# Storing the attention outputs of the first two sequences at other steps of the item loop

## The chip, the cores and the metric

The kernel runs on one core of a Trainium2 chip. The metric is the device time of one execution in microseconds (us); the time given for a kernel is the median of its runs.

## What is computed

The reference is an attention block of the RWKV-5 kind (a recurrent state for each head, decayed by w at each token) followed by a mixture of experts that uses one expert for a token. Cut to what matters:

```python
# r, k, v: (B, H, S, D) = (4, 8, 768, 48); w, u: (H, D)
for t in range(S):
    cur = einsum('bhd,bhe->bhde', u * k[t], v[t])
    y[t] = einsum('bhd,bhde->bhe', r[t], state + cur)
    state = w * state + einsum('bhd,bhe->bhde', k[t], v[t])
x = y as (B, S, H * D)                      # 4 x 768 tokens of 384
logits = x @ w_gate                         # 8 experts
e[s] = argmax(logits[s]) if s == 0 or sigmoid(x[s] @ w_local) < 0.5 else e[s - 1]
out[s] = softmax(logits[s])[e] * (relu(x[s] @ w1[e]) @ w2[e])
```

x, the attention's output, is the array whose storing the change moves. The kernel keeps it in device memory as `x_d` (3072 rows of 384 float32), because the experts later gather its rows by token number.

## The kernel before

**Stages.** First comes attention (0 to about 107 us), with the routing of the first two sequences woven in; then the experts (to the end of the span at 380 us), with the routing of the other two woven into the first expert units. The order of the work on each engine is written out by hand: the program is emitted under `manual_schedule`, and each engine runs its instructions in the order of the code. The framework adds the semaphores.

**Items and steps.** Attention works on 16 items, an item being one sequence b and one pair of heads hp (n = 4 b + hp). `Attention.run` (L352) is a loop over steps n = 0 to 16. A regular step does, in this order: `load(n + 3)` puts three DMAs on SP's queue (rk, kv and vT of a later item); `turn(n - 2)` transposes the outputs of item n - 2 on TensorE and copies them on ScalarE (ACT) into the tile `x` of their sequence (L329, L331); `added` and `states` form the states between chunks; `scale(n + 1)` is three multiplies on GpSimd (POOL), rw, ke and pd; `inside(n - 1)` and `before(n - 1)` finish the products of item n - 1 on TensorE, and `before` ends with one ACT copy from PSUM into `xT` (L318); two calls of `scores` (L288) and their masking on VectorE (DVE, L290) follow for the item ahead; `own(n)` (L267, L273) begins the outputs of item n in PSUM; `keys` is one more DVE multiply. Where n is a multiple of 4, `logits` (L342, L343) multiplies the gate's weights with the outputs of the sequence that has just been finished.

**Where the stores are.** An item's outputs are turned two steps after its own, so the four items of sequence b are all in `x` after `turn` of step 4 b + 5. There, at the end of `turn`, L334 stores the whole sequence, 768 rows of 1536 bytes, with one DMA on ACT's queue: for the first sequence in step 5, the second in step 9, the third in step 13, the fourth after the loop. ACT issues it right after the copies that it depends on.

**Buffers.** `x` has two buffers (L305): the third sequence's tile is the first's again, and the fourth's is the second's. The first write into the third sequence's tile is the pair of copies of `turn(8)` in step 10, into the fourth's that of `turn(12)` in step 14. These copies have to wait until the store that reads the old contents has landed. The PSUM for the transposes comes from two pairs of banks that every user takes in turn (`banks`, L184): in a regular step `turn` takes one, the first `scores` the other, the second `scores` the first one again. The outputs of `own` have a single tile `y`, which the ACT copy into `xT` must have read before `own` of the next item writes it.

**Loads.** Four buffers each hold rk and vT and five hold kv, so SP issues a load as soon as its buffer is free, up to three steps ahead of the loop.

**Readers of x_d.** `heads()` in step 15 is the first gather (L1083, POOL), from the rows of the first two sequences. Later gathers read all rows.

Of the kernel before, what the change touches and what calls it, by code (L numbers as in the profile page):

```python
# [20 lines left out]
P = 128  # L21
B, H, S, DH = 4, 8, 768, 48
HP = H // 2
# [38 lines left out]
class Attention:  # L62
# [260 lines left out]
    def turn(self, n, banks):  # L323

        nc, b, h0 = self.nc, self.items[n]["b"], 2 * self.items[n]["hp"]
        x = self.xs[b]
        for h in range(2):
            for c2 in range(C2):
                nc.tensor.transpose(banks[h][:, c2 * P:c2 * P + U], self.outputs(b, h0 + h)[:U, c2 * P:(c2 + 1) * P], self.ident[:U, :U])  # L329
        for h in range(2):  # L330
            nc.scalar.copy(x[:, :, (h0 + h) * DH:(h0 + h + 1) * DH],  # L331
                           banks[h][:, :C2 * P].rearrange("p (c e) -> p c e", e=DP)[..., :DH])
        if h0 == H - 2:
            nc.scalar.dma_start(out=self.x_d[b * S:(b + 1) * S, :].rearrange("(c p) d -> p c d", p=P), in_=x)  # L334

    def logits(self, b, bank):

# [14 lines left out]
    def run(self, router, fetch, heads):  # L352
# [11 lines left out]
        for n in range(M + 1):  # L364
# [69 lines left out]
            if n == g + 3:  # L434

                router.turn_runs(0, mp[:, mp_end:])
            self.before(n - 1)
            if M - 2 <= n < M:
                fetch(2 * (n - M + 2) + 1)
            if n == 6:  # L440
# [478 lines left out]
def route(tc, once, ps, lt, ident, gates):  # L919
# [57 lines left out]
    nc.vector.tensor_copy(ccol, cp[:NC, :1])  # L977
    run = tl("run", [NC, P])
    nc.vector.tensor_tensor_scan(run, rows, rows, ccol, Alu.max, Alu.max)
    rp = bank("rp")  # L980
    nc.tensor.transpose(rp[:, :NC], run, ident[:NC, :NC])
    ei = tl("ei", [P, NC], I32)
    nc.vector.tensor_copy(ei, rp[:, :NC])
# [15 lines left out]
class Experts:  # L999
# [49 lines left out]
    def fetch(self, i, engine):  # L1049
        u, wp = self.units[i], self.wps[i % 2]  # L1050
        if i < EARLY:
            w1, w2 = self.w1[u["e"]], self.w2[u["e"]]
        else:
            e = self.nc.values_load(self.router.order[0:1, i - EARLY:i - EARLY + 1], engines=[ET.SP], min_val=0, max_val=E - 1,
                                    skip_runtime_bounds_check_because="the blocks' experts are a permutation")
            w1, w2 = [w[bass.ds(e, 1)].rearrange("o p x -> (o p) x") for w in (self.w1, self.w2)]
        u["w1"] = wp.tile([P, FK, DK, P], F32, name="w1t", tag="w1t")
        engine.dma_start(out=u["w1"].rearrange("p m k f -> p (m k f)"), in_=w1)
        u["w2"] = wp.tile([P, FK, D], F32, name="w2t", tag="w2t")
        engine.dma_start(out=u["w2"].rearrange("p m f -> p (m f)"), in_=w2)  # L1060
# [691 lines left out]
```

## Time and profile before

| what | us |
|---|---|
| median of three runs | 381.67 (381.08 to 381.85) |
| the profiled execution, whole | 382.02 |
| its span, first to last instruction | 380.2 |
| PE busy in the span | 366.5 (96%) |
| DVE, POOL, ACT busy | 249.2, 151.2, 107.2 |
| ACT starts to issue the four stores at | 40.35, 64.70, 90.31, 114.80 |
| one issue on ACT | 0.38 to 0.40 |
| `before`'s ACT copy (L318) of steps 8, 9, 10, 12 starts at | 59.73, 67.34, 72.62, 84.46 |
| copies of `turn(8)`, `turn(12)` start at | 69.83, 94.96 |
| first gather starts at | 106.41 |

How to read it: PE is TensorE's matmuls, PEld its weight loads, DVE VectorE, ACT ScalarE, POOL GpSimd, SP the engine that issues the loads. A line of the timeline has the start, the duration, engine and source line, the operation with its output and input tiles, how many, and in square brackets how long the engine sat idle before and what ended that. A line of the waits has the waiting instruction, what it waited for, the total in us, how often, and the longest. The rows of slices cut the span into 40 equal parts of 9.5 us and give a busy share in tenths. "DMA to landing" is the time from the issue of a DMA to its completion. The DMA queues are told apart too: q1 holds SP's loads, q10 the DMAs that ACT issues.

### The profile page before, as it was taken

To read this page: it belongs to the slowest core of one execution; us is meant where nothing else is said; L and a number is where in the kernel's file an instruction comes from. 1 tells how busy PE (TensorE), PEld (TensorE's weight loads), DVE (VectorE), ACT (ScalarE), POOL (GpSimd) and SP (SyncE) were. 2 spreads that over 40 slices of the span, in tenths; PEclk is the share of its full clock that TensorE was granted. 3 is DMA by queue.
4 is the path that set the end of the run, shared out by engine and by line. 5 is a ranking of instruction groups with operands and counts; after the bars stand their busy time and mean duration, and the time that the engine had idled before them with its cause. 6 is when DMAs were issued, how large, how long until landed. Compare 5 with 4: busy or idle time off the path is not lost. (4 is left out here: it accounts for less than half of the span.)

```text
span 380.2 us, 9697 instructions
## 1 busy us (share of the span) xinstructions
PE 366.5 (96%) x3846; PEld 323.6 (85%) x3846; DVE 249.2 (66%) x720; ACT 107.2 (28%) x295; POOL 151.2 (40%) x213
## 2 busy tenths in 40 slices
PE   8899999999999999999999999999999999999992
PEld 7676777776769989999999999999898899899971
DVE  6988778889853736587557857757658758466400
ACT  4132232232322112223323233233233233232210
POOL 7699999896222043211423213223323123012022
PEclk9999999999999999999999999999999999999997
DMA  7999999973738872811561254146146156063011
GB/s 255 413 411 407 409 395 338 378 276 128 246 121 288 331 275 72 320 53 39 202 219 42 68 222 174 35 174 228 56 167 232 34 181 228 12 225 161 3 37 36
DMA packets 17765, 74.97 MB, mean 197 GB/s; under 512 B 2761, under 2 KB 6618, under 8 KB 15408
## 3 DMA queue, kind: packets, MB, share of 16 engines
q1 hardware_dynamic: 10336, 56.89, 40.0%
q0 software_dynamic: 3424, 9.52, 7.5%
q10 hardware_dynamic: 3952, 7.87, 5.8%
q8 instruction: 32, 0.52, 0.6%
q14 instruction: 21, 0.17, 0.2%
HBM read 64.83 MB, written 9.51 MB: 196 GB/s over the span
## 5 line engine op out<-in xcount | busy, mean ns | idle before, releaser
L1309 POOL DMA_INDIRECT out_dram<-yo,sid x27 | 26.6, 986 | 102.2 <-ACT yo L1304 78.7
L1160 PE MATMUL h<-exT,w1t 128*128 128x168 f32 (+4 forms) x240 | 54.9, 327 | 0.0
L1164 DVE TENSOR_TENSOR hT<-h,hs 128x168 f32<-128x168 f32 (+3 forms) x60 | 21.1, 351 | 46.1 <-PE h L1160 30.5
L1083 POOL DMA_INDIRECT xg<-x_d,gid x29 | 31.2, 1076 | 36.2 <-DVE sm L906 17.4
L1160 PEld LDWEIGHTS h<-exT,w1t 128*128 128x128 f32 x240 | 41.6, 190 | 0.3 <-issue 0.3
L1110 PE MATMUL h<-exT,w1t 128*128 128x192 f32 (+1 forms) x192 | 38.3, 338 | 0.0
L1229 PE MATMUL y<-factors,sums 128*128 128x192 f32 x168 | 36.8, 326 | 0.0
L290 DVE TENSOR_TENSOR am<-pair,kept 128x768 f32<-128x768 f32 x32 | 29.9, 952 | 8.9 <-PE pair L288 8.7
L1160 PE MATMUL h<-xs,ws 128*128 128x168 f32 (+4 forms) x144 | 35.2, 326 | 0.0
L216 POOL TENSOR_TENSOR pd<-rk 128x384 f32<-128x384 f32 x32 | 31.4, 1003 | 7.7 <-PE y L267 5.5
L1110 PEld LDWEIGHTS h<-exT,w1t 128*128 128x128 f32 x192 | 32.3, 190 | 1.5 <-issue 0.2
L1160 PEld LDWEIGHTS h<-xs,ws 128*128 128x128 f32 x144 | 25.5, 190 | 4.3 <-ACT hs L1167 1.0
L1229 PEld LDWEIGHTS y<-factors,sums 128*128 128x128 f32 x168 | 28.9, 190 | 0.0
L212 POOL TENSOR_TENSOR ke<-kv,endT 128x288 f32<-128x288 f32 x32 | 24.9, 800 | 1.8 <-DMA kv<-in_kv_dram 1.8
L297 PE MATMUL y<-am,kv 128*64 128x128 f32 x360 | 22.8, 276 | 1.3 <-DVE y L273 1.2
L229 POOL TENSOR_TENSOR rw<-rk,tab 128x384 f32<-128x384 f32 x26 | 23.7, 936 | 0.2 <-DMA rk<-in_rk_dram 0.2
L288 PE MATMUL pair<-rw,kw 48*64 48x128 f32 (+1 forms) x768 | 23.0, 249 | 0.4
L1229 PE MATMUL y<-w2t,hT 128*128 128x192 f32 x96 | 23.0, 328 | 0.0
L1097 DVE COPY exT<-tp 128x384 f32<-128x384 f32 (+6 forms) x29 | 14.0, 489 | 13.6 <-PE tp L1096 13.4
L288 PEld LDWEIGHTS pair<-rw,kw 48*64 48x64 f32 x768 | 19.5, 133 | 2.6 <-POOL ke L212 0.6
L318 ACT COPY xT<-y 128x768 f32<-128x768 f32 x15 | 12.0, 799 | 33.6 <-PE y L310 33.6
L297 PEld LDWEIGHTS y<-am,kv 128*64 128x64 f32 x360 | 19.4, 137 | 2.4 <-DVE y L273 1.7
(301 smaller groups left out, 739.2 us busy)
## 6 DMA issues: line engine op xcount, KB each, us to landing
w1t<-in_w_dram SPq DMA_DIRECT2D x8, 1536.0 KB, 6.7
w2t<-in_w_dram SPq DMA_DIRECT2D x8, 1536.0 KB, 7.2
rk<-in_rk_dram SPq DMA_DIRECT2D x15, 768.0 KB, 9.1
kv<-in_kv_dram SPq DMA_DIRECT2D x16, 584.0 KB, 7.9
vT<-in_vT_dram SPq DMA_DIRECT2D x16, 384.0 KB, 10.0
x_d<-x ACTq DMA_DIRECT2D x4, 1152.0 KB, 9.5
w1t<-in_w_dram SPq DMA_DIRECT2D x2, 768.0 KB, 5.9
w2t<-in_w_dram SPq DMA_DIRECT2D x2, 768.0 KB, 5.4
```

The source lines that it names most:

```text
L212: nc.gpsimd.tensor_mul(t["ke"][:, p::2], t["k"][:, p::2], spread(self.endT[:, p, hp], 1, C2))
L216: nc.gpsimd.tensor_mul(t["pd"][:, z], t["rT"][:, z], t["kT"][:, z])
L229: engine.tensor_mul(t["rw"][:, z], t["rT"][:, z], spread(pw, 1, z.stop - z.start))
L288: nc.tensor.matmul(sc[f * DP:(f + 1) * DP, h, i, x:], lhsT=t["kw"][q, c, o * DP:(o + 1) * DP], rhs=t["rw"][q, c, x:], start=True, stop=True)
L290: return lambda: nc.vector.tensor_mul(t["am"][:, g], sc, spread(self.kept[:, g:g + 3], 1, 2))
L297: nc.tensor.matmul(t["y"][h][p * DP:(p + 1) * DP, c2 * P:(c2 + 1) * P], lhsT=t["v"][:, (2 * c + h) * DH:(2 * c + h) * DH + DP], rhs=t["am" ...
L1083: self.nc.gpsimd.indirect_dma_start(out=xg[:n], out_offset=None, in_=self.x_d[:rows], in_offset=bass.IndirectOffsetOnAxis(ap=u["gid"][:n, ...
L1110: nc.tensor.matmul(h[:, :n], lhsT=u["w1"][:, m, kk, :], rhs=u["xT"][:, kk, :], start=(kk == 0), stop=(kk == DK - 1))
L1160: nc.tensor.matmul(out, lhsT=a, rhs=b, start=start and k == 0, stop=stop and k == len(terms) - 1, skip_group_check=True)
L1164: nc.vector.tensor_tensor(out, a, b, op=Alu.add)
L1229: return lambda: nc.tensor.matmul(bank[:, x * half:(x + 1) * half], lhsT=a, rhs=b, start=(j == 0 and x == 0), stop=(j == FK // 2 - 1), ski ...
L1309: self.nc.gpsimd.indirect_dma_start(out=out.rearrange("n (h d) -> (n h) d", h=2) if half else out, out_offset=bass.IndirectOffsetOnAxis(ap ...
```

## The change

The store is taken out of `turn` into a function of its own, and `turn` calls it for the third and the fourth sequence alone. In the steps n = 8 and n = 12 the loop calls it, right after `before(n - 1)`, for the sequences 0 and 1. So the first sequence's store moves from step 5 to step 8, the second's from step 9 to step 12, both still on ACT's queue, now behind the copy into `xT` (L318) and ahead of the one of `logits` (L343). No instruction is added or taken away.

```diff
@@ turn
             nc.scalar.copy(x[:, :, (h0 + h) * DH:(h0 + h + 1) * DH],
                            banks[h][:, :C2 * P].rearrange("p (c e) -> p c e", e=DP)[..., :DH])
-        if h0 == H - 2:
-            nc.scalar.dma_start(out=self.x_d[b * S:(b + 1) * S, :].rearrange("(c p) d -> p c d", p=P), in_=x)
+        if h0 == H - 2 and b >= 2:
+            self.store(b)
+
+    def store(self, b):
+        self.nc.scalar.dma_start(out=self.x_d[b * S:(b + 1) * S, :].rearrange("(c p) d -> p c d", p=P), in_=self.xs[b])
@@ run
             self.before(n - 1)
+            if n in (2 * HP, 3 * HP):
+                self.store(n // HP - 2)
```

## Prediction

> **What bounds the kernel now.** I read the page's slices first, then busy time by stretch, the waits, and at last the timelines of ACT and PE around the places where the stores stand and where they are to go. The page's rows for TensorE and the DMA engines (40 slices of 9.5 us):
>
> ```profile
> PE   8899999999999999999999999999999999999992
> DMA  7999999973738872811561254146146156063011
> ```
>
> TensorE is nine tenths busy nearly from start to end, so anything that stops it shows in the time. The DMA engines are full only up to about 85 us, the attention stage, in which the four stores to x_d lie. Busy time by stretch there (one step of the loop is some 5.5 us; columns: length, busy us of PE, PEld, DVE, ACT, POOL, clock, DMA share, GB/s):
>
> ```profile
> 33.00:39.60 6.60, 6.26 (x149) 3.97 (x147) 5.03 (x7) 1.28 (x2) 6.60 (x9) 1.00 1.02 409
> 39.60:45.80 6.20, 6.14 (x132) 4.79 (x132) 4.00 (x24) 1.52 (x4) 6.20 (x8) 1.00 1.02 407
> 56.90:64.00 7.10, 7.10 (x148) 4.83 (x149) 6.20 (x8) 2.01 (x5) 7.10 (x9) 1.00 0.95 349
> 64.00:69.80 5.80, 5.80 (x131) 4.53 (x131) 3.27 (x8) 1.64 (x4) 4.13 (x6) 1.00 0.95 337
> 69.80:75.75 5.95, 5.95 (x149) 4.85 (x151) 5.88 (x11) 1.50 (x3) 5.95 (x8) 1.00 1.03 388
> 81.70:89.60 7.90, 7.90 (x168) 5.75 (x169) 6.94 (x10) 2.24 (x6) 7.49 (x9) 1.00 0.24 82
> ```
>
> Up to 64 us GpSimd has no idle time at all, from 57 us on TensorE has none; ACT is idle three quarters of the time. The clock is 1.00 throughout. From 40 us on no engine waits for a load: the last such wait is in the stretch 28 to 40 us, before the first store is issued,
>
> ```profile
> POOL ke L212 <- DMA kv<-in_kv_dram: 0.7, 1, 0.7
> ```
>
> So in these stretches the DMA engines are full, but not the bound. The issue of the first store, and landings in us by stretch, in an answer for 40 to 41 us and one for 80 to 100 us:
>
> ```profile
> L334 ACTq DMA_DIRECT2D x_d<-x x1: 400/400/400, 40.4 to 40.4; - x1
> DMA to landing us min/median/max: 14.4/14.4/14.4
> ```
> ```profile
> L334 ACTq DMA_DIRECT2D x_d<-x x1: 378/378/378, 90.3 to 90.3; - x1
> DMA to landing us min/median/max: 4.6/4.6/4.6
> ```
>
> The same 1152 KB take 14.4 us among loads and 4.6 us alone. That spread is what this change turns on.
>
> **What is taken out at steps 5 and 9.** Two issues, 0.40 us at 40.35 and 0.39 us at 64.70 on ACT. Behind them ACT is idle until 43.28 and 66.18, waiting for PE and DVE, so nothing is late there: gain 0. Their transfers leave two full stretches. The loads get about 3 us of DMA time back in 40 to 55 us (1.18 MB at 0.41 MB/us), but no one waits for them there, and GpSimd, which sets the pace, does the same 5.5 us of multiplies for an item: 0. One wait of SP's own is tied to the first store: in 50 to 55 us SP waits 0.8 us for x_d before a vT issue, and then 2.5 us more for a DVE multiply at L273 which is to free the buffer, so that too is worth 0. An upper bound for what I do not see: TensorE's idle time between 39.6 and 85 us. By stretch it is 0.06, 0.12, 0.12, 0, 0, 0 and 0.59 us, to 81.7 us; if all 0.9 us went, that would be the gain.
>
> **What is added at step 12.** The second store is issued after the copy at 84.46, so at 85.26. ACT's next work is at 87.43, after 2.17 us of waiting for PE, which hides the 0.4 us. From 85 to 90 us the DMA share is 0.01, so the price is that of the store at 90.31: landing at 85.26 + 4.6 = 89.9. Its buffer is written again by the copies at 94.96 (step 14, the first of the fourth sequence), 5.1 us later, and the gather that reads x_d starts at 106.41. Cost 0. Only the 14.4 us row would be too late here, by 99.7 - 94.96 = 4.7 us, and the reason for that row, the loads, is gone by then.
>
> **What is added at step 8.** This is the part that can cost. ACT's lines from the step 8 copy to the step 10 copies, and PE's of step 10:
>
> ```profile
> 59.73 0.80 ACT L318 COPY xT<-y 128x768 f32<-128x768 f32 x1 [2.09 <-PE y L310]
> 63.26 0.48 ACT L343 COPY lT<-pair 128x384 f32<-128x384 f32 x1 [2.73 <-PE pair L342]
> ...
> 69.83 0.70 ACT L331 COPY x<-pair 128x288 f32<-128x288 f32 x2 [1.69 <-PE pair L329]
> 72.62 0.80 ACT L318 COPY xT<-y 128x768 f32<-128x768 f32 x1 [2.09 <-PE y L310]
> ```
> ```profile
> 69.00 0.79 PE L329 MATMUL pair<-ident,xT 112*128 112x112 f32 x6
> ...
> 72.31 1.27 PE L288 MATMUL pair<-rw,kw 48*64 48x128 f32 x46
> 73.47 0.88 PE L267 MATMUL y<-pd,w_t 48*64 48x384 f32 x8
> ```
>
> The issue falls at 59.73 + 0.80 = 60.53, into 2.73 us in which ACT waits for PE: 0.4 us, hidden. But x has two buffers. The copies at 69.83 are the first to write the third sequence's rows, into the buffer that the first store reads. At present that store has landed at 54.8; now it must land within 9.3 us. If it has not, the copies wait on ACT, and behind them the xT copy of 72.62.
>
> How late may it land for nothing? The copies take 0.70 us. The xT copy ends at 73.42 and PE's L267 at 73.47 overwrites what it reads, so the copies must end by 72.62 + 0.05, that is start by 71.97. The copies' own PSUM pair is written again by the second half of the 48 score matmuls that run from 72.20 to 73.47, at about 72.8, so start by 72.1. The nearer limit is **72.0 us**. Each us after it is one us of TensorE, for from 70 to 80 us PE has no idle time, and DVE and POOL hardly any to make it up (4.93 and 5.00 of the first 5 us).
>
> When does it land? Ends: 60.53 + 4.6 = 65.1 (no loads) and 60.53 + 14.4 = 74.9 (loads all the time). Between them I go by the queue rows of 2 us windows. Loads use 95, 88, 81, 83 and 10% of the engines in the windows from 60, 62, 64, 66 and 68 us, and 70% from 70 us. The store needs 1.18 MB at 0.74 MB in 2 us (the third store's rate in 92 to 94 us), 3.2 us of all engines. The second store, issued at 64.70, has its first packets after 66 us, so I start at 62.7. Free time is then 0.15 + 0.38 + 0.35 + 1.79 = 2.7 us up to 70.0, and the last 0.5 us takes until 71.7, at 30% free. Two things pull at this: the loads before it will run up to 3 us earlier, with the first store gone from 40 to 55 us; but a store's last packets come late (the second has 457 packets in 68 to 70 us and still 12 in 74 to 76 and 3 in 76 to 78, which is 11.3 to 13.3 us after its issue). I take **71.5 us, give or take one**: ACT waits 1.7 us, TensorE does not. The ends of the cost are 0 and 74.9 - 72.0 = 2.9 us.
>
> [...]
>
> SP's queue: some eight issues after the store, a load may wait for it, as vT did at 57.29. Now that is the issue at 75.48 or 75.90, after any landing I reckon with. Loads beside the store have room: rk issued at 63.32 is first used by DVE at 81.61.
>
> **Sum.** 0 + 0 + 0 + 0 = no change, with TensorE 0.5 us away from a loss. The profiled execution took 382.02 us (span 380.2 and 1.8 around it), 0.35 above the median 381.67 of the runs. I forecast 381.8 against that median: 0.1 is the share of landings slightly past 72.0.
>
> **Rivals.**
> 1. *The store lands too late for its buffer (slower).* The wait at L331 in step 10 goes beyond 72.0. By the 12.2 us middle of the second store's end it lands at 72.7 and costs 0.7 us (382.4); by the first store's 14.4 us, 2.9 us (384.6). It decides from 72.0 on, and becomes visible past 72.8. For it: two of the three stores with a visible end took 11 us or more, both beside loads. Against it: the lightly loaded window at 68 to 70 us.
> 2. *The full DMA stretch gets relief (faster).* If the stores hold up something that the views do not show (instructions being fetched, the loads' landing), up to 0.9 us comes back, 380.8. Against it: no engine waits for a load after 40 us.
> 3. *Hidden both before and after, with the time moved by less than 0.2%*: this is the forecast.
>
> **How the numbers follow.** About 0.2% (0.76 us) is what a measurement of this kernel can tell from no change. Forecast, landing up to 72.7: 0.50, 381.4 to 382.4. Rival 1 beyond that: 0.34, 382.4 to 384.6, more of it at the low end. Rival 2: 0.16, 380.8 or a little less. The range 380.8 to 383.5 leaves out the late third of rival 1 and a little of rival 2.
>
> **What would show it.** Right: the store's issue at about 60.5 in ACT's empty 2.7 us; an ACT wait for x_d before L331 in step 10, with landing before 72; PE without a gap from 69 to 80 us; the second store alone in 85 to 90 us, landing in about 4.6. Wrong: a PE wait for ACT at L288 or L267 near 73 us (rival 1), or shorter steps between 40 and 60 us (rival 2).

## The result, and the profile after

The changed kernel takes 384.25 us (median of 18 runs, 382.34 to 387.57) against 381.96 (18 runs, 381.08 to 383.77) beside it: ratio 1.0055, 95% interval 1.0037 to 1.0072. It is slower, by 2.1 us going by the ratio, and the time of a single run is spread twice as wide as before. Ratios, here and below, are estimated from the fast runs alone and are not the quotient of the two medians. The profiled execution took 385.49 us with a span of 383.7; that of before was 382.02 and 380.2, so this one lost 3.5 us. Rival 1 of the prediction came true, in the upper half of its band.

The profile's rows after (slices of 9.6 us): the clock has two slices below 9, the second of them the last of the span, and the DMA row has moved its idle part.

```profile
PE   8899999699989999999999999999999999999992
...
PEclk9999999989999999999999999999999999999997
DMA  7999999956765880830551155145246146064011
```

The dip of PE in slice 8 (67 to 77 us) and the 8 of the clock in slice 9 mark the loss. ACT's timeline from step 8 to step 10, start, duration, line, and idle time with its cause:

```profile
59.20 0.80 ACT L318 COPY xT<-y 128x768 f32<-128x768 f32 x1 [2.09 <-PE y L310]
59.26 0.40 ACTq L337 DMA_DIRECT2D x_d<-x  x1
62.42 0.48 ACT L346 COPY lT<-pair 128x384 f32<-128x384 f32 x1 [2.42 <-PE pair L345]
...
66.53 0.80 ACT L318 COPY xT<-y 128x768 f32<-128x768 f32 x1 [1.04 <-PE y L310]
74.50 0.70 ACT L331 COPY x<-pair 128x288 f32<-128x288 f32 x2 [7.17 <-DMA x_d<-x]
75.09 0.82 ACT L318 COPY xT<-y 128x768 f32<-128x768 f32 x1
```

The issue itself is hidden as reckoned; it even starts beside the copy, not behind it. But the copies of step 10 sit for 7.17 us until the store has landed, 15.2 us after its issue. PE in the same step:

```profile
71.91 0.71 PE L288 MATMUL pair<-rw,kw 48*64 48x128 f32 x22
75.35 0.95 PE L288 MATMUL pair<-rw,kw 48*64 48x128 f32 x24 [2.72 <-ACT x L331]
75.96 1.62 PE L267 MATMUL y<-pd,w_t 48*64 48x384 f32 x8
77.51 1.04 PE L248 MATMUL mp<-kv,ke 128*48 128x48 f32 x20
```

The gap stands at the second of the two limits that the prediction names, the one for the PSUM pair: between the two score calls, because the second needs the pair that the copies have not read. What follows is slower too: L267 takes 1.62 us in place of 0.88, L248 1.04 in place of 0.65. The line of L248 in the kernel before:

```profile
74.28 0.65 PE L248 MATMUL mp<-kv,ke 128*48 128x48 f32 x20
```

Busy time by stretch after (length, busy us of PE, PEld, DVE, ACT and POOL, clock, DMA share, GB/s):

```profile
72.00:75.00 3.00, 0.62 (x28) 0.49 (x20) 2.18 (x3) 0.50 (x2) 2.24 (x3) 1.00 1.03 406
75.00:76.00 1.00, 0.65 (x26) 0.65 (x28) 0.00 (x0) 0.91 (x2) 0.00 (x0) 0.90 0.94 389
76.00:79.00 3.00, 3.00 (x38) 1.73 (x32) 1.07 (x2) 0.00 (x0) 1.27 (x2) 0.50 0.17 68
79.00:80.00 1.00, 1.00 (x14) 0.86 (x14) 1.00 (x3) 0.29 (x1) 1.00 (x2) 0.89 0.31 61
```

After the gap the clock is at half speed for more than 3 us. The account, from the starts of the L318 copies of each step, before and after: step 5 begins its copy 0.15 us earlier; steps 6 to 9 are shorter by 0.10, 0.29, -0.01 and 0.28 us; step 10 is 3.28 longer (8.56 for 5.28), step 11 1.49 longer (7.08 for 5.59); step 12 gets 0.60 back, step 14 loses 0.11. Sum 3.5 us, the whole difference of the spans. The second store, at 87.89, costs nothing that these lines show.

The granted clock of the single runs fits the same half speed outside the profile. It is 0.993 to 0.997 in the runs of the kernel before that were measured beside the experiments. Of the 18 runs of the changed kernel, nine have 0.994 to 0.997 and take 382.34 to 384.37 us, the other nine 0.987 to 0.992 and 384.12 to 387.57.

### The profile page after: what moved, and what is told of

The parts are those of the page before. It is cut to its first block, busy times and chain, and to the rows that moved or that the text cites. A ratio compares the mean times of both kernels' runs of the same rounds, so it can differ in the third digit from the quotient of the medians.

```text
span 383.7 us, 9698 instructions
## 1 busy us (share of the span) xinstructions
PE 367.7 (96%) x3846; PEld 324.7 (85%) x3846; DVE 249.2 (65%) x720; ACT 107.1 (28%) x295; POOL 151.3 (39%) x213
## 5 line engine op out<-in xcount | busy, mean ns | idle before, releaser
L288 PE MATMUL pair<-rw,kw 48*64 48x128 f32 (+1 forms) x768 | 23.3, 250 | 3.0 <-ACT x L331 2.7
L288 PEld LDWEIGHTS pair<-rw,kw 48*64 48x64 f32 x768 | 19.6, 133 | 5.3 <-issue 3.5
L318 ACT COPY xT<-y 128x768 f32<-128x768 f32 x15 | 12.0, 801 | 31.4 <-PE y L310 31.4
```

Source lines behind the costliest of these rows:

```text
L288: nc.tensor.matmul(sc[f * DP:(f + 1) * DP, h, i, x:], lhsT=t["kw"][q, c, o * DP:(o + 1) * DP], rhs=t["rw"][q, c, x:], start=True, stop=True)
```

## The experiments

All ratios are to the kernel before, run on the same chip beside each kernel, with 95% intervals. The edits are against the changed kernel, cut to the lines that matter. Theory A is the wait for the buffer. The rivals are B, contention of the store with other traffic, C, the second store's move, and from the first results on D, a loss of PE beside a store among the loads that no wait in the profile shows.

**Only the second store moved** (`second_only`):

```diff
-        if h0 == H - 2 and b >= 2:
+        if h0 == H - 2 and b != 1:
-            if n in (2 * HP, 3 * HP):
+            if n in (3 * HP,):
```

> Only the second store is moved (step 9 to step 12); the first stays in step 5. Theory A (the loss comes from the copies of step 10, which wait for the first store to leave the buffer): no wait there, ratio to the kernel before 1.000 within 0.002. Theory B (stores beside loads cost by contention, wherever they stand): one store fewer among the loads of 64 to 77 us, ratio at or a little below 1.000. Theory C (the second store's move is what costs): ratio 1.003 to 1.006, with the loss after 85 us.

Measured: 381.94 us, ratio 0.9992 (0.9979 to 1.0004). C falls. Its profiled execution (384.06 us, the slowest of its twelve runs) shows something else, in two steps alike; PE's timeline in step 7:

```profile
51.12 0.29 PE L248 MATMUL mp<-kv,ke 128*48 128x48 f32 x3
52.08 0.57 PE L248 MATMUL mp<-kv,ke 128*48 128x48 f32 x17 [0.67 <-issue]
```

A run of 20 like matmuls stops after three of them for 0.67 us, and no engine or DMA that the profile shows is what it waits for. One packet of the instruction queue falls between 49 and 50 us; whether the stop has to do with it is not shown. The first store's transfer was under way then; it landed at 53.3, ahead of the second such stop, which ends at 58.20.

**Only the first store moved** (`first_only`): the first store in step 8, the second left in `turn`.

```diff
-        if h0 == H - 2 and b >= 2:
+        if h0 == H - 2 and b != 0:
-            if n in (2 * HP, 3 * HP):
+            if n in (2 * HP,):
```

> Only the first store is moved (step 5 to step 8); the second stays in step 9, so two stores are under way at once from 64 us. Theory A: the first store lands later than the 74.4 us of the changed kernel's profile, as the second shares the engines, at 75 to 78; PE waits 3 to 6 us in step 10; ratio 1.006 to 1.015. Theory C: ratio 1.000.

Measured: 384.83 us, ratio 1.0077 (1.0049 to 1.0106), six runs from 382.79 to 387.24. The profiled execution is the quickest of the six. PE's line there:

```profile
73.68 0.77 PE L288 MATMUL pair<-rw,kw 48*64 48x128 f32 x24 [0.84 <-ACT x L331]
```

The copies start at 72.83 here, 13.3 us being the time to landing, and a gap of 0.84 us is all; the clock stays at 1.00. So my expectations of a landing at 75 to 78 and of a wait of 3 to 6 us were too high for this execution. The loss of the others was not seen in a profile, but the four slowest of the six have a granted clock of 0.989 to 0.991, the profiled one 0.996. The first store's move alone gives the loss.

**The wait taken away** (`third_buffer`): the third sequence's x lies in the memory of an expert weight tile that is loaded later; the stores stand as in the change.

```diff
+            if t["b"] == 2:
+                self.xs[2] = self.wp0.tile([P, FK, D], F32, name="w2t", tag="w2t")[:, :NCH]
+            else:
                 self.xs[t["b"]] = self.late.tile([P, NCH, D], F32, name="x", bufs=2)
```

> The changed kernel, but the third sequence's x lies in memory of its own (that of the expert weights loaded later), so no copy has to wait for the first store; the stores stand where the change put them. Theory A: no wait for x_d on ACT, no gap on PE at 72 to 75 us, clock 1.00, ratio 1.000 within 0.002, while the first store still lands at about 74. Theory B: ratio stays at 1.004 to 1.007, as the traffic is the same.

Measured: 382.64 us, ratio 1.0006 (0.9991 to 1.0021). The store, issued at 59.05, still takes as long, and the copies of step 10 no longer mind:

```profile
DMA to landing us min/median/max: 14.5/14.5/14.5
```
```profile
69.18 0.70 ACT L334 COPY w2t<-pair 128x288 f32<-128x288 f32 x2 [2.05 <-PE pair L332]
71.96 0.80 ACT L321 COPY xT<-y 128x768 f32<-128x768 f32 x1 [2.08 <-PE y L313]
```

The store at the same place, no wait, and the loss is gone but for what the interval allows (0.21%, 0.8 us): this decides for A as the cause. B is not nothing, though. In this profile steps 6 to 9 are 0.66 us shorter than before, as in the changed kernel, and steps 10 and 11 are 0.35 and 0.92 us longer, with stops of PE whose cause no engine shows, such as

```profile
73.73 0.87 PE L267 MATMUL y<-pd,w_t 48*64 48x384 f32 x7 [0.39 <-issue]
```

So in these profiles the store among the loads has a price of its own, here paid in another place than before.

**The first store on SP's queue** (`sp_queue`):

```diff
-        self.nc.scalar.dma_start(
+        (self.nc.sync if b == 0 else self.nc.scalar).dma_start(
```

> The changed kernel with the first store issued by SP, in step 8's place of SP's own order, that is behind the loads of item 11 and ahead of those of item 12, at about 57 us. Theory A, with landing set by the later loads that share the engines: nothing later is taken ahead of it in its queue, landing by 66 us, no wait in step 10, ratio 1.000 within 0.002. If a store is slow among loads whatever its queue, it lands 12 to 15 us after its issue, at 69 to 72, so just in time, with ratio 1.000 to 1.003.

Measured: 382.71 us, ratio 1.0012 (0.9999 to 1.0025), issue at 57.2, copies of step 10 at 69.27 without a wait for x_d. Both parts of the expectation allow this time, and no row gives the landing. The sizes of the packets tell it nearly: the store's rows are 1536 bytes, and in the kernel before no packet of 62 to 64 us, when SP's queue moved loads only, lies between 512 B and 2 KB. Here, for 60 to 62, 62 to 64 and 64 to 66 us:

```profile
DMA packets 489, 0.78 MB, mean 390 GB/s; under 512 B 5, under 2 KB 465, under 8 KB 489
DMA packets 336, 0.83 MB, mean 416 GB/s; under 512 B 14, under 2 KB 263, under 8 KB 336
DMA packets 188, 0.83 MB, mean 416 GB/s; under 512 B 24, under 2 KB 29, under 8 KB 187
```

These are 460, 249 and 5 such packets; with 54 in 58 to 60 us they are the 768 rows of the store, the last of them before 65 us. The store was through 7.8 us after its issue, so the first part of the expectation holds and the second does not: on ACT's queue the same store took 13 us and more.

**One step earlier** (`step7`):

```diff
-            if n in (2 * HP, 3 * HP):
-                self.store(n // HP - 2)
+            if n in (2 * HP - 1, 3 * HP):
+                self.store((n + 1) // HP - 2)
```

> The changed kernel with the first store one step earlier, after the copy of step 7, at about 54 us. Theory A: landing after the 14 to 15 us seen among loads, at 68 to 70, ahead of the copies at 69; no wait beyond 72; ratio 1.000 within 0.002. If the wait in the changed kernel has another cause than the time from issue to landing, ratio 1.004 to 1.007 as before.

Measured: 382.93 us, ratio 1.0008 (0.9993 to 1.0024), issue at 54.18 and

```profile
DMA to landing us min/median/max: 13.4/13.4/13.4
```

so 67.6, ahead of the copies. As expected by A. Eleven of the twelve runs lie between 381.51 and 383.61 us; the other took 387.55 at a granted clock of 0.987, like the slowest runs of the changed kernel, and is not in the ratio.

**One step later** (`step9`): the first store after the copies of `turn` in step 9.

```diff
+                if n == 2 * HP + 1:
+                    self.store(0)
-            if n in (2 * HP, 3 * HP):
+            if n in (3 * HP,):
```

> The changed kernel with the first store later, after the copies of turn in step 9, at about 63 to 64 us, 4.5 us later than in step 8. Theory A: landing 10 to 15 us after the issue, at 73 to 78; PE waits 1 to 6 us in step 10, and after a gap of 2 us and more runs at half clock for about 3 us (0.50 in the changed kernel's profile); ratio 1.008 to 1.020, more than the changed kernel's 1.0055. If it is the step 8 place that costs (contention there), ratio at most 1.0055.

Measured: 391.10 us, ratio 1.0183 (1.0140 to 1.0225). Issue at 62.95, copies at 79.63, 16.7 us later. PE, and the stretches in its gap and behind it:

```profile
80.47 1.33 PE L288 MATMUL pair<-rw,kw 48*64 48x128 f32 x24 [8.49 <-ACT x L331]
```
```profile
76.00:80.00 4.00, 0.00 (x0) 0.00 (x0) 0.00 (x0) 0.37 (x2) 0.00 (x0) 0.56 0.18 71
80.00:82.00 2.00, 1.53 (x28) 1.39 (x32) 0.00 (x0) 1.03 (x3) 0.00 (x0) 0.50 0.00 0
82.00:84.00 2.00, 2.00 (x29) 0.90 (x22) 0.82 (x1) 0.00 (x0) 0.77 (x1) 0.50 0.03 8
84.00:86.00 2.00, 2.00 (x15) 1.72 (x15) 1.74 (x4) 0.47 (x2) 2.00 (x4) 0.50 0.41 97
86.00:88.00 2.00, 2.00 (x35) 1.80 (x35) 1.08 (x3) 0.40 (x2) 2.00 (x4) 0.82 1.04 419
```

With step 7 at 1.0008, step 8 at 1.0055 and step 9 at 1.0183 the loss follows the time of issue, as a deadline would have it. The wait was longer than the 1 to 6 us expected, because the landing took 16.6 us, not 10 to 15, and the half speed lasted 10.2 us by these rows, not about 3.

**TensorE kept busy in the gap** (`warm_wait`): 12 transposes between the two score calls of step 10.

```diff
                 self.scores(ahead, 0)()
+                if n == 10:
+                    for _ in range(12):
+                        self.nc.tensor.transpose(mp[:, P + 1:2 * P + 1], self.ident, self.ident)
```

> The changed kernel with 12 transposes of the identity into an unused part of PSUM between the two score calls of step 10, where PE waits; they keep TensorE busy for about 1.6 us. Theory A with a clock part (after the 2.7 us gap the clock was 0.50 from 76 to 79 us, about 1.4 us of the loss): the idle part of the gap falls to about 1 us, the clock stays at 1.00, the wait stays; ratio 1.001 to 1.004. If the clock plays no part: the wait is as long, ratio 1.0055 or above.

Measured: 383.90 us, ratio 1.0044 (1.0027 to 1.0061). The stretches in its profile:

```profile
72.00:76.00 4.00, 2.94 (x58) 2.23 (x49) 1.86 (x3) 1.40 (x3) 1.93 (x3) 1.00 0.96 384
76.00:80.00 4.00, 4.00 (x80) 3.28 (x72) 3.51 (x6) 0.87 (x3) 3.45 (x4) 1.00 0.47 158
```

The gap still holds 1.1 us of idle time in two pieces, the clock stays at 1.00, and step 11 takes 5.60 us where the changed kernel's took 7.08 and the kernel before 5.59: in the profile the 1.5 us are gone. Step 12 takes 6.17 for 5.65, so about 1.0 us of them is left over both steps. All seven runs have a granted clock of 0.994 to 0.997, so by the clock the half speed is gone from the timed runs too. Their time does not show it: the ratio lies just above the expected 1.001 to 1.004, and beside 1.0055 and 1.0043 (`change_again`) for the change. The edit has a price of its own: the transposes wait 0.77 us for a DVE scan and take 1.53, so the second score call would come some 2.3 us late even if the store had landed; the quickest run took 383.66 us, where the change has 382.20. So the clock part is shown, and its size in time rests on one profile against another.

**The change once more** (`change_again`), the same code:

> The changed kernel once more, for a second sample of the landing. Theory A: the copies of step 10 wait for x_d again, landing 12 to 16 us after an issue at about 59; ratio 1.004 to 1.007, with a spread of runs wider than that of the kernel before, as the landing varies from run to run and the loss begins only beyond about 72. If the first profile's wait was an accident of that execution: no wait, ratio near 1.000.

Measured: 384.03 us, ratio 1.0043 (1.0025 to 1.0060), 12 runs from 382.20 to 384.97. Landing, PE's line and four stretches:

```profile
DMA to landing us min/median/max: 14.0/14.0/14.0
```
```profile
74.07 1.17 PE L288 MATMUL pair<-rw,kw 48*64 48x128 f32 x24 [1.79 <-ACT x L331]
```
```profile
74.00:75.00 1.00, 0.93 (x27) 0.96 (x31) 0.00 (x0) 0.62 (x1) 0.00 (x0) 0.64 0.98 377
75.00:76.00 1.00, 1.00 (x13) 0.27 (x5) 0.00 (x0) 0.00 (x0) 0.00 (x0) 0.50 0.88 363
76.00:77.00 1.00, 1.00 (x18) 0.55 (x16) 0.39 (x1) 0.00 (x0) 0.33 (x1) 0.50 0.28 96
77.00:78.00 1.00, 1.00 (x19) 0.91 (x16) 0.74 (x2) 0.00 (x0) 1.00 (x2) 0.65 0.00 0
```

The wait is no accident. A landing 1.4 us earlier than in the first profile (73.1 for 74.5) shortens the gap by 0.9 us, and half clock comes here too, after a gap of 1.8 us. Steps 11 and 12 take 7.07 and 5.65 us, as in the first profile.

**Half the store** (`half_store`): three chunks of tokens in step 5, three in step 8.

```diff
+        if h0 == H - 2 and b == 0:
+            self.store(b, 0, C2)
-                self.store(n // HP - 2)
+                self.store(n // HP - 2, C2 if n == 2 * HP else 0)
```

> The first store is cut in two: its first three chunks of tokens are stored in step 5, the other three in step 8; the second store in step 12. Theory A: the transfer of step 8 has 576 KB instead of 1152, so its last packets come 3 to 6 us earlier, at 68 to 71; no wait of PE, ratio 0.999 to 1.002. If it is the start behind loads already issued that makes it late, and not its size (about 5 us pass from issue to the first packets in the changed kernel), it lands at 72 to 74 and the ratio is 1.002 to 1.005.

Measured: 381.91 us, ratio 1.0002 (0.9992 to 1.0012). Issue of the second half at 59.68 and

```profile
DMA to landing us min/median/max: 8.5/8.5/8.5
```

so 68.2, without a wait. Half the bytes land 5.5 to 6.7 us sooner than the whole (14.0 and 15.2).

**Both stores after the loads** (`late_both`): with the third buffer of above, both in step 12.

```diff
-            if n in (2 * HP, 3 * HP):
-                self.store(n // HP - 2)
+            if n == 3 * HP:
+                self.store(0)
+                self.store(1)
```

> As third_buffer, but the first store is issued in step 12 too, right ahead of the second, when all loads of the items have been issued and the DMA engines are nearly idle; x of the fourth sequence takes the first's buffer, which must be free at about 94. Theory A alone: no wait, as in third_buffer, ratio 1.000 within 0.002. [...]

Measured: 381.71 us, ratio 0.9987 (0.9974 to 0.9999). In ACT's and PE's timelines:

```profile
83.46 1.00 ACTq L340 DMA_DIRECT2D x_d<-x  x2
```
```profile
45.34 0.91 PE L248 MATMUL mp<-kv,ke 128*48 128x48 f32 x20
...
50.83 0.66 PE L248 MATMUL mp<-kv,ke 128*48 128x48 f32 x20
...
56.11 0.66 PE L248 MATMUL mp<-kv,ke 128*48 128x48 f32 x20
```

The same three runs in the kernel before:

```profile
45.67 1.01 PE L248 MATMUL mp<-kv,ke 128*48 128x48 f32 x20
...
51.27 0.98 PE L248 MATMUL mp<-kv,ke 128*48 128x48 f32 x20
...
56.83 0.66 PE L248 MATMUL mp<-kv,ke 128*48 128x48 f32 x20
```

The first store lands in 4.7 us; the landing of the second is not shown. The third sequence's store, issued at 89.31, takes 6.4 us.

**The same once more** (`late_again`):

> late_both once more, as its ratio of 0.9987 lies close to 1. [...]

Measured: 381.45 us, ratio 0.9991 (0.9982 to 1.0000). Twice about 0.1% faster than the kernel before, each time with the interval's end at 1: the best version of this study, by some 0.4 us if the gain is one. Its profile has one gap that the kernel before has not, 0.73 us with no cause shown, in L288 at 79 us, with no store under way.

## Why the prediction was wrong

The forecast was no change, 381.8; the measured ratio on its 381.67 makes 383.8, beyond the range's 383.5 and inside rival 1.

- *Issues, SP's queue, second store:* right. ACT's waits took in the issues; `second_only` is at 0.9992.
- *The limit of 72.0 us:* right to 0.1 us. The one that acted was the second of the two, the PSUM pair at 72.1, because the second score call comes ahead of L267 in the order of PE. The changed kernel ran 0.4 us ahead at step 10, so 71.7 there; a landing at 74.5 gives 2.8 us, and PE's gap was 2.72.
- *The landing at 71.5:* this step failed. It was 74.5 and 73.1, at 15.2 and 14.0 us from issue, against the 11 of the estimate, though the issue came at 59.26, 1.3 us ahead of the 60.53 reckoned. I filled the store into the free time of the queue rows of before. Those rows again for 68 to 70 us, which I had counted as nine tenths free, first before, then after (packets, MB, share of the engines):

```profile
q10 hardware_dynamic: 457, 0.70, 93.0%
q1 hardware_dynamic: 18, 0.09, 10.4%
```
```profile
q1 hardware_dynamic: 126, 0.65, 78.2%
q10 hardware_dynamic: 125, 0.19, 25.4%
```

  The window was nearly free of loads before because nothing had held them up. Now the store took its share from 64 us on: the loads got 39.4 and 68.7% of the two windows from 64 and 66 us, for 80.9 and 82.6% before. They moved back into this window, and the store got a quarter of it. Nor did the store start at 62.7: two packets went before 64 us. The nearest row, 14.4 us for the same store among loads, was better than the finer sum: 13.1 to 16.6 us in the nine profiles here in which a whole store's landing among loads on ACT's queue is shown. On SP's queue, where 460 of the 489 packets of 60 to 62 us were the store's, it was through in 7.8 us (`sp_queue`).
- *One us for each us beyond the limit:* too little. Behind gaps of 1.79 and 2.72 us PE ran at half clock for 3.4 us. Step 11 paid 1.49 us for it. Step 12 got 0.60 of that back: PE had been idle there for 0.59 us before, which stands in the prediction's list of idle times up to 81.7 us, but behind the 80 us at which its rule stops.
- *Rival 2, relief:* it exists, though I gave it no more than a sixth. From the L318 copy of step 5 to that of step 9 it takes 24.06 us before and 25.53 in `second_only`, with the first store issued in step 5; 24.14 with it in step 7; 23.34 to 23.40 in all nine profiles with it in step 8 or later. So the store cost 0.7 us or more in steps 5 and 7, and one that is moved among other loads takes a price along (0.35 and 0.92 us in `third_buffer`); only `late_both` takes it out of the loads. The prediction's argument, that no engine waits for a load there, holds; what lost time was PE, in stops with no cause shown, of 0.67 us each in `second_only`.
- *The spread:* the chance of 0.34 for slower was put on an uncertainty that a kernel shows from run to run: the landing differs between executions (74.5 and 73.1 in the two profiles), and the loss sets in only past the limit. The two groups of granted clocks, with nine runs each, fit this; the landing of an execution without a profile is not known.

## What to carry to other kernels

A store has a deadline as soon as its buffer is written again, and moving it later spends slack that no busy row shows (15 us before, from the landing at 54.8 to the copies at 69.83): find the next writer, then who waits behind it. For a transfer among others take the time of a like transfer among others (14.4 us before, 15.2 and 14.0 after), not the free share of a profile without it (11 us), since the traffic that it displaces comes back to take that share (the loads took 10.4% of the window from 68 to 70 us before, 78.2% after); or put it on the queue of the loads, ahead of the next ones, as `sp_queue` did at a ratio of 1.0012 (0.9999 to 1.0025). Price a gap of TensorE above its length where the profile's clock falls behind it (here 0.50 for 3.4 us, and 1.49 us more in step 11); the first store was cheapest here where the loads had ended and its buffer stayed untouched, in `late_both` (landing in 4.7 us, ratio 0.9987). What PE lost beside a store among loads, 0.7 us or more in steps 5 and 7, is no such wait, and here it moved with the store.

## What the runs showed of the hardware

- A gap of PE of 0.84 us left the clock at 1.00 (`first_only`), gaps of 1.79 (`change_again`), 2.72 (the changed kernel) and 8.49 us (`step9`) were followed by 0.50, in the first two of these three setting in only after matmuls had begun again. The half speed lasted 3.4 us behind the gaps of 1.79 and 2.72, and 10.2 us around the end of the gap of 8.49, three times as long (estimates from the clock of the rows of 1 to 4 us, taken as either 1.00 or 0.50).
- Runs of like matmuls stop in the middle for 0.2 to 0.7 us with no cause shown. Two of these stops, of 0.67 us each in `second_only`, end at 52.08 and 58.20 us; a packet of the instruction queue falls between 49 and 50 us and another between 55 and 56, but no run shows that the stops come from them. Many stops came with a store among the loads, and went where the store had gone (L248 at 51 us: 0.98 us before, 0.66 in `late_both`), but not all (L248 at 45 us: 1.01 and 0.91; the stop of `late_again`).
- The same store of 768 rows needed 13.1 to 16.6 us among loads on ACT's queue, 4.6 to 6.4 us behind the last loads of the items, and 7.8 us at most on the queue that the loads themselves use: from 60 to 62 us 460 of 489 packets were the store's.
